# Rotating batch 0 at once, spreading the first weight conversion, and 512-token expert passes after attention

## The chip, the core and the metric

The kernel runs on one core of a Trainium2 chip. The metric is the device time of one execution in microseconds.

## The reference

Attention with rotary embedding, then two feed-forward layers ("expert layers") over the same 2304 tokens. All inputs are float32 but the four weight matrices, which arrive as 64-bit floats.

```
q, k, v: (4 batches, 8 heads, 576 positions, 64)
rotate(x) = concat(x1*cos - x2*sin, x1*sin + x2*cos)
attn = softmax(rotate(q) @ rotate(k).T / 8); o = attn @ v
x  = o.transpose(0, 2, 1, 3).reshape(2304, 512)
h  = x @ w_in1;  x2 = (s * relu(h)**2 + b) @ w_out1      # w_in1 (512, 2048), w_out1 (2048, 512)
h2 = x2 @ w_in2; out = (h2 * sigmoid(1.702 * h2)) @ w_out2
```

## The kernel before

Precision is kept by splitting: each weight, each activation tile x and each hidden tile g is held as a high part and a low part, and each product is made of three matmuls (high by high, high by low, low by high). A weight matrix pair is cut into 16 pieces f of 128 hidden columns; a piece has two halves, m = 0 of `w_in` and m = 1 of `w_out`, 512 KB of 64-bit floats each. `make_half` loads a half into a staging tile and converts it: one ScalarE scaling (L400), three VectorE integer instructions (L401, L402, L405) that put a float32 together out of the two words, a ScalarE cast that gives the high part (L408) and a GpSimd subtraction that gives the low part (L409). Layer 0 keeps 11 converted pieces in SBUF (`HELD`, tags `w0` to `w10`); the other five (`STREAMED`: 2, 5, 8, 11, 14) are converted into one shared buffer (`ws0`, `ws1`), spilled to DRAM and fetched again in every pass. Layer 1 keeps all 16: five in room that is free after attention, the others in the tiles of layer 0's pieces as these are let go.

Work is put into slots. A slot is one score tile of attention; there are 144, 36 for each batch, and some slots below 0 for the preparation. `at(slot, fn)` files a task; a loop at the end goes through the slots, sets a priority of 1000 for each slot, and calls the tasks. The order in which each engine's queue then holds the instructions is laid out by a planner when the kernel is built, by these priorities and a model of when inputs are ready; TensorE's order alone is that of the program (`pin`).

Batch 0 is prepared below slot 0. For each of four head pairs p, and for k and q, `rope_load` fetches a tile `nat` (two buffers shared by all), `rope_cross`, `rope_mul` and `rope_add` rotate it, on GpSimd for k and for most q, on VectorE for q with p < `RV`; `rope_turn` transposes it on TensorE in two groups, splits it into `z` and spills it to DRAM, from where `fetch_pair` brings it back in the layout of the scores. `plan_rope` files pair p's load at slot -16 + 4p and its turns from four slots on. `plan_scales` loads v (`vm`) and makes its scales. The conversion of layer 0's piece f is filed at slot `CONV[0] + CONV[1] * f` = -12 + f.

In a slot, four matmuls make the scores, VectorE copies them out with their minimum (L301), ScalarE takes the exponential, GpSimd normalizes (L321), TensorE transposes, ScalarE and VectorE make the two parts (below slot 20 TensorE and ScalarE, `rest_tile`), and after each four or five slots `weighted` multiplies by v and stores to DRAM (`xT`).

The expert layers run as a generator, `experts`, over passes of 256 tokens: nine for layer 0, nine for layer 1. A step is `first_layer` (FL: 12 matmuls, four chunks by three products, then ScalarE and VectorE make g) or `second_layer` (SL: for layer 0, 12 matmuls of 256 columns; for layer 1, 6 of 512), SL two steps of f behind FL (`SKEW`). From slot 22 on, when the tokens of the first pass are there (`avail`), `target` says how many steps are to be taken in each slot, so that layer 0's passes 0 to 6 lie among attention's slots; the last 512 tokens need the end of attention. Then `widen` gives attention's SBUF and PSUM to the experts, the rest of layer 0 runs, and `refill` converts layer 1's pieces, one for each step, in order of f: the first `EARLY` ones at once, each other one when SL of layer 0's last pass has let a held piece go. `prepare` loads a pass's x and splits it, `finish` copies a pass's sums out and stores them.

## Time and profile before

| | us |
|---|---|
| median of 3 runs (1332.11 to 1335.58) | 1332.78 |
| the profiled execution | 1331.08 |
| its span | 1329.2 |
| TensorE busy | 1133.8 (85%) |
| VectorE busy | 757.0 (57%) |
| ScalarE busy | 684.1 (51%) |
| GpSimd busy | 353.0 (27%) |

The profile is of one execution; times in it count from the start of its span. Busy times are of instructions at work; a matmul's end is modelled, and matmuls are pipelined, so that the distance from one group of matmuls to the next tells more than a matmul's own length. PE is TensorE, PEld its weight load, DVE VectorE, ACT ScalarE, POOL GpSimd, SP the engine whose queue issues the DMAs; L12 is line 12 of the kernel.

### The profile page before, as it was taken

The page shows a single profiled execution, that of the slowest core. Times are in us where ns is not written, and L with a number is a line of the kernel's source. Part 1 is how long each engine was busy: PE and PEld are TensorE (multiplying, and loading weights), DVE is VectorE, ACT ScalarE, POOL GpSimd, SP SyncE. Part 2 cuts the span into 40 slices and gives each one's busy share as a digit, 9 for nine tenths or more (in the row PEclk, how much of TensorE's full clock was granted, in tenths as well). Part 3 has the DMA queues.
Part 4 walks back from the last instruction along what each step waited for, and adds up shares of the span by engine and source line. Part 5 has one row for each costly group of instructions (what it writes and reads, how often), then busy time and mean ns, then how long its engine had stood idle before and what let it go on. Part 6 is the DMA issues. An engine that isn't in the chain of part 4 may idle for free.

```text
span 1329.2 us, 23590 instructions
## 1 busy us (share of the span) xinstructions
PE 1133.8 (85%) x8584; PEld 1046.5 (79%) x8584; DVE 757.0 (57%) x1652; ACT 684.1 (51%) x1483; POOL 353.0 (27%) x350
## 2 busy tenths in 40 slices
PE   0126568998999999899999968987999999999998
PEld 0124448887889889898899968987899999999997
DVE  7888736766566676576665649389333333333322
ACT  2348555666566666566666647566333323332332
POOL 5675644432424343244111113044000000000000
PEclk9998689999989999999999989999999999999999
DMA  7987746657755677475665357566011101100000
GB/s 243 302 278 248 245 137 177 198 169 241 220 166 180 192 247 226 151 210 173 195 212 161 112 168 248 165 223 190 16 33 32 31 2 33 32 17 17 17 17 17
DMA packets 133204, 197.42 MB, mean 149 GB/s; under 512 B 32352, under 2 KB 99424, under 8 KB 133088
## 3 DMA queue, kind: packets, MB, share of 16 engines
q1 hardware_dynamic: 133088, 195.91, 47.8%
q8 instruction: 68, 1.11, 0.4%
q14 instruction: 48, 0.39, 0.1%
HBM read 152.34 MB, written 43.52 MB: 147 GB/s over the span
## 4 chain that ended last, share of the span: by engine, by line
PE 55%; DMA 12%; issue 11%; DVE 10%; ACT 5%; POOL 4%; SPq 2%; DVEq 0%; POOLq 0%; ACTq 0%
PE acc L90 21%; PE l L90 14%; PE l1b L90 7%; PE t L90 4%; PE av L90 4%; PE s L90 4%; DVE P L301 2%; POOL w L409 2%; DMA xT<-pt 2%; DMA vm<-in_v_dram 2%; DMA stage<-in_moe_w_out_dram 2%; DMA xl0b<-xT 1%; DVE pt L344 1%; DMA qb<-qsp 1%; ACT P L310 1%
## 5 line engine op out<-in xcount | busy, mean ns | idle before, releaser
L321 POOL TENSOR_SCALAR P<-P,st 128x576 f32<-128x576 f32 x144 | 113.9, 792 | 344.4 <-DVE st L320 244.7
L90 PE MATMUL acc<-w,gh1b 128*128 128x512 f32 x576 | 202.4, 392 | 0.0
L310 ACT ACTIVATE P<-P,st 128x576 f32<-128x576 f32 x144 | 111.8, 776 | 103.8 <-DVE P L301 103.8
L90 PE MATMUL acc<-gh0b,w 128*128 128x256 f32 x792 | 164.8, 290 | 0.1
L90 PE MATMUL l<-xh0b,w 128*128 128x256 f32 x704 | 145.6, 289 | 14.0 <-ACT r0b L505 8.7
L90 PE MATMUL t<-ident,P 128*128 128x128 f32 x720 | 109.1, 285 | 45.4 <-ACT pt L359 24.8
L301 DVE TENSOR_SCALAR_CACHE_REDUCE P<-s 128x576 f32<-128x576 f32 x144 | 108.5, 753 | 63.5 <-PE s L90 62.2
L90 PEld LDWEIGHTS acc<-gh0b,w 128*128 128x128 f32 x792 | 131.4, 193 | 1.1 <-issue 0.7
L409 POOL TENSOR_TENSOR w<-stage,w 128x512 fp32r<-128x512 f32 x64 | 92.6, 1450 | 145.4 <-ACT w L408 139.6
L90 PEld LDWEIGHTS l<-xh0b,w 128*128 128x128 f32 x704 | 117.9, 195 | 16.0 <-ACT r0b L505 10.4
L90 PEld LDWEIGHTS t<-ident,P 128*128 128x128 f32 x720 | 84.2, 145 | 58.4 <-issue 23.0
L90 PE MATMUL s<-k,qb 128*128 128x288 f32 x640 | 121.3, 317 | 3.9 <-DVE P L301 3.9
L90 PEld LDWEIGHTS acc<-w,gh1b 128*128 128x128 f32 x576 | 108.8, 189 | 19.3
L90 PE MATMUL l<-xh1b,w 128*128 128x256 f32 x576 | 115.1, 283 | 4.4 <-DVE r1b L510 4.4
L90 PE MATMUL l1b<-xh1b,w 128*128 128x256 f32 x576 | 115.1, 283 | 3.7 <-DVE r1b L510 3.7
L344 DVE TENSOR_TENSOR pt<-t,pt 128x640 f16<-128x640 f32 x124 | 101.9, 822 | 28.4 <-ACT pt L342 28.0
L90 PE MATMUL acc<-gl0b,w 128*128 128x256 f32 x396 | 113.1, 286 | 2.9 <-DVE gl0b L514 2.9
L90 PE MATMUL acc<-w,gl1b 128*128 128x512 f32 x288 | 113.8, 395 | 0.0
L342 ACT CAST pt<-t 128x640 f16<-128x640 f32 x144 | 99.0, 688 | 18.6 <-PE t L90 17.4
L90 PEld LDWEIGHTS s<-k,qb 128*128 128x128 f32 x640 | 95.5, 198 | 12.5 <-issue 6.7
L507 ACT ACTIVATE r0b<-r0b,sb 128x256 f32<-128x256 f32 x144 | 86.8, 603 | 33.0 <-DVE r0b L506 32.6
L90 PE MATMUL l<-xl0b,w 128*128 128x256 f32 x352 | 101.5, 288 | 1.4 <-DVE xl0b L479 0.7
(97 smaller groups left out, 2564.5 us busy)
## 6 DMA issues: line engine op xcount, KB each, us to landing
ws<-wd SPq DMA_DIRECT2D x90, 512.0 KB, 4.5
k<-ksp SPq DMA_DIRECT2D x32, 576.0 KB, 5.8
stage<-in_moe_w_in_dram SPq DMA_DIRECT2D x32, 512.0 KB, 4.7
stage<-in_moe_w_out_dram SPq DMA_DIRECT2D x32, 512.0 KB, 4.4
ksp<-z SPq DMA_DIRECT2D x32, 160.0 KB, 4.6
qsp<-z SPq DMA_DIRECT2D x32, 160.0 KB, 4.4
wd<-w SPq DMA_DIRECT2D x10, 512.0 KB, 5.4
vsp<-vz SPq DMA_DIRECT2D x16, 320.0 KB, 4.6
```

The costliest lines, as they stand in the source:

```text
L90: pin(nc.tensor.matmul(*args, **kw))
L301: nc.vector.tensor_scalar(pr.rearrange("p (n s) -> p n s", n=2), ps[:, :, :HS], -Q_SCALE, None, op0=ALU.mult, op1=ALU.min, accum_out=st[:, ...
L310: nc.scalar.activation(pr, pr, AF.Exp, bias=st[:, 0:1], scale=-1.0, accum_out=st[:, 1:2])
L321: nc.gpsimd.tensor_scalar(pr, pr, st[:, 2:3], 1.0, op0=ALU.mult, op1=ALU.mult)
L342: nc.scalar.copy(hi, pc)
L344: nc.vector.tensor_tensor(lo, pc, hi, op=ALU.subtract)
L409: nc.gpsimd.tensor_tensor(lo, f32(low), f32(hi), op=ALU.subtract)
L507: nc.scalar.activation(r, r, AF.Identity, bias=sb[:, 1:2], scale=sb[:, 0:1])
```

## The change

Two things are changed together.

At the start: all tiles of batch 0's rotation are loaded one after the other (pair p at slot -16 + p) and each pair has a tile of its own, `boot`, that holds natural q and k and k's cross products; it lies in the room of weight pieces that are converted later. The turns of pair p are filed at slots 4p - 8 to 4p - 6. `RV` is 3. The conversion of piece f is filed at slot -4 + 2f, its cast and its subtraction one slot later (`WLAG`); the staging tiles of the pieces below 13 lie in the room of the last two held pieces.

After attention: layer 0's last two passes become one of 512 tokens, layer 1 has four passes of 512 and a last one of 256. FL and layer 0's SL then have 512 columns in a matmul. Layer 1 streams pieces 11 and 14 and holds 14, of which three go ahead; a streamed piece is fetched two steps of f ahead (`EARLIER`), and its conversion waits until the shared buffer is let go (`freed[1]`). PSUM has five accumulator banks in a ring and three FL banks (before: six and two).

```diff
-    STREAMED = ((2, 5, 8, 11, 14), ())
+    STREAMED = ((2, 5, 8, 11, 14), (11, 14))
-    EARLY = NF - len(HELD[0])
+    EARLY = len(HELD[1]) - len(HELD[0])
...
+    boot = {}
+    BOOT = (5, 6, 7, 8)
...
+    def boot_part(p, i):
+        return boot[p][:, i * S : (i + 1) * S].rearrange("p (t e i) -> p t e i", t=RT, e=2)
     def rope_load(b, p, which, st):
-        nat = att.tile([128, RT, 2, HD], F32, tag="nat", name=f"nat{b}{p}{which}")
+        if b == 0:
+            if p not in boot:
+                boot[p] = wpool.tile([128, 2048], F32, tag=f"w{BOOT[p]}", name=f"boot{p}")
+            nat = boot_part(p, which)
+        else:
+            nat = att.tile([128, RT, 2, HD], F32, tag="nat", name=f"nat{b}{p}{which}")
...
     def make_half(t, w_in, w_out, f, m, nm):
+        elif f < HELD[0][-2]:
+            if m == 0:
+                stages[0] = wpool.tile(
+                    [128, 2, 512], U64, tag=f"w{len(HELD[0]) - 1 - f % 2}", name=f"stage{nm}"
+                )
+            raw = stages[0][:, m]
...
-        nc.scalar.copy(hi, f32(low))
-        nc.gpsimd.tensor_tensor(lo, f32(low), f32(hi), op=ALU.subtract)
+        def split():
+            nc.scalar.copy(hi, f32(low))
+            nc.gpsimd.tensor_tensor(lo, f32(low), f32(hi), op=ALU.subtract)
+        return split
...
-        make_half(t, *W[layer], f, m, f"{layer}_{f}")
+        split = make_half(t, *W[layer], f, m, f"{layer}_{f}")
+        if layer == 0:
+            at(int(CONV[0] + CONV[1] * f) + WLAG, split)
+        else:
+            split()
...
+        pool = late["acc"] if ring[0] % 5 in (1, 2, 3) else ps_acc
...
+    PASSES = [(0, t, TB) for t in range(0, NT - 2 * TB, TB)] + [(0, NT - 2 * TB, 2 * TB)]
+    PASSES += [(1, t, 2 * TB) for t in range(0, NT - TB, 2 * TB)] + [(1, NT - TB, TB)]
+    LAST0 = [n for n, x in enumerate(PASSES) if x[0] == 0][-1]
...
     def experts():
...
-            while late and len(kept[1]) < NF:
-                f = len(kept[1])
+            while late and turned[0] < NF:
+                f = turned[0]
                 if f in HELD[1]:
                     if HELD[1].index(f) >= freed[0]:
                         break
...
                     if not freed[1]:
                         break
                     freed[1] = 0
-                for m in range(2):
-                    weight(1, f, m)
-                fresh[f] = kept[1][f]
+                fresh[f] = [weight(1, f, m) for m in range(2)]
+                turned[0] += 1
                 return
...
-            if (layer, blk) == (0, NB - 1) and f in HELD[0]:
+            if n == LAST0 and f in HELD[0]:
                 freed[0] += 1
-            if (layer, blk, f) in [(0, NB - 1, NF - 1)] + [(1, 0, x) for x in STREAMED[1]]:
+            if (n, f) in [(LAST0, NF - 1)] + [(LAST0 + 1, x) for x in STREAMED[1]]:
                 freed[1] = 1
...
+                z = f + EARLIER
+                if late and z in STREAMED[layer] and z not in fresh and n != LAST0 + 1:
+                    fetched[z] = fetch_weight(layer, z, f"{n}_")
...
-        gap = 2 if b else 1
         for g in range(2):
-            at(s + 4 + gap * g, rope_turn, b, p, which, g, st)
+            at(s + 4 + 2 * g if b else 4 * p + RT0 - which + g, rope_turn, b, p, which, g, st)
...
-    CONV = (-12, 1.0)
+    CONV = (-4, 2)
+    RT0 = -7
+    WLAG = 1
...
-    RV = 2
+    RV = 3
...
-                r = bounds[b - 1] + RS + 9 * p if b else -RL + 4 * p
+                r = bounds[b - 1] + RS + 9 * p if b else -RL + p
...
-        late["acc"] = ctx.enter_context(tc.tile_pool(name="ps_acc2", bufs=4, space=PSUM))
+        late["acc"] = ctx.enter_context(tc.tile_pool(name="ps_acc2", bufs=3, space=PSUM))
```

## Rows read from the trace of the kernel before

**Rows 1.** Windows: stretch, its length, each engine's busy us (instructions), granted clock, DMA share, GB/s.
```profile
0.00:70.00 70.00, 10.10 (x35) 5.68 (x35) 57.93 (x83) 24.30 (x42) 41.55 (x39) 1.00 0.84 276
70.00:160.00 90.00, 43.27 (x227) 32.12 (x227) 73.90 (x131) 55.13 (x105) 64.60 (x53) 0.83 0.80 257
160.00:192.00 32.00, 18.69 (x153) 14.15 (x151) 11.03 (x40) 18.87 (x36) 14.07 (x16) 0.93 0.64 182
...
217.00:767.00 550.00, 511.71 (x4437) 488.91 (x4436) 355.26 (x885) 346.37 (x764) 180.33 (x204) 0.98 0.63 190
...
794.00:905.00 111.00, 102.41 (x814) 99.87 (x815) 81.15 (x134) 72.27 (x148) 31.53 (x23) 0.98 0.64 211
905.00:936.00 31.00, 22.73 (x154) 20.01 (x153) 28.80 (x44) 18.41 (x38) 11.68 (x10) 1.00 0.58 181
936.00:1324.00 388.00, 387.98 (x2469) 351.90 (x2468) 123.95 (x281) 122.77 (x298) 1.30 (x1) 1.00 0.08 20
```

**Rows 2.** Groups by line, VectorE, 0 to 192 us.
```profile
L402 DVE SCALAR_TENSOR_TENSOR stage<-stage 128x512 uint32<-128x512 uint32 x32 | 34.4, 1075 | 5.7 <-ACT stage L400 4.7
L405 DVE SCALAR_TENSOR_TENSOR stage<-stage 128x512 uint32<-128x512 uint32 x32 | 34.1, 1064 | 0.5
L401 DVE TENSOR_SCALAR stage<-stage 128x512 uint32<-128x512 uint32 x32 | 26.1, 816 | 0.0
```

**Rows 3.** Windows of line L405 alone: VectorE busy us (instructions).
```profile
0.00:70.00 70.00, 15.96 (x14) 1.00 0.84 276
70.00:160.00 90.00, 18.09 (x18) 0.83 0.80 257
```

**Rows 4.** Timeline of TensorE: start, length, what, count, idle time before it.
```profile
56.21 1.11 PE L93 MATMUL r<-ident,nat 128*128 128x128 f32 x4 [9.97 <-POOL nat L205]
...
69.93 1.30 PE L90 MATMUL s<-k,qb 128*128 128x288 f32 x4
...
160.26 1.31 PE L90 MATMUL s<-k,qb 128*128 128x288 f32 x4
...
185.53 0.80 PE L90 MATMUL s<-k,qb 128*128 128x288 f32 x4
191.70 0.58 PE L90 MATMUL l<-xh0b,w 128*128 128x256 f32 x1 [5.37 <-ACT xh0b L478]
```

**Rows 5.** Timeline of GpSimd, the first rotation.
```profile
7.89 1.81 POOL L197 TENSOR_TENSOR rot<-nat,tab 128x288 f32<-128x288 f32 x2 [6.59 <-DMA nat<-in_k_dram]
...
11.36 1.79 POOL L205 TENSOR_TENSOR nat<-nat,rot 128x576 f32<-128x576 f32 x1
```

**Rows 6.** DMA issues, 0 to 192 us: count, KB each, median us to landing.
```profile
stage<-in_moe_w_in_dram SPq DMA_DIRECT2D x16, 512.0 KB, 4.9
...
wd<-w SPq DMA_DIRECT2D x10, 512.0 KB, 5.4
```

**Rows 7.** Timeline of VectorE, the first conversions.
```profile
11.82 1.62 DVE L401 TENSOR_SCALAR stage<-stage 128x512 uint32<-128x512 uint32 x1
...
14.03 0.68 DVE L402 SCALAR_TENSOR_TENSOR stage<-stage 128x512 uint32<-128x512 uint32 x1
14.63 0.41 DVE L401 TENSOR_SCALAR stage<-stage 128x512 uint32<-128x512 uint32 x1
14.97 0.68 DVE L405 SCALAR_TENSOR_TENSOR stage<-stage 128x512 uint32<-128x512 uint32 x1
```

**Rows 8.** Chain that ended last, in layer 1: start, length, what.
```profile
1301.52 1.43 PE l L90 x12
1302.95 1.39 PE acc L90 x6
```

**Rows 9.** Timeline of GpSimd after attention.
```profile
826.86 1.31 POOL L409 TENSOR_TENSOR w<-stage,w 128x512 fp32r<-128x512 f32 x1 [1.67 <-ACT w L408]
863.29 4.24 POOL L409 TENSOR_TENSOR w<-stage,w 128x512 fp32r<-128x512 f32 x3 [35.12 <-ACT w L408]
```

**Rows 10.** Timeline of TensorE, after attention's last matmuls.
```profile
794.26 0.55 PE L90 MATMUL l1b<-xh0b,ws 128*128 128x256 f32 x1 [10.62 <-DMA ws<-wd]
```

More of the change, by code (lines that the diff above doesn't have):

```diff
@@ L400, in make_half @@
         nc.scalar.activation(f32(high), f32(high), AF.Copy, scale=2.0**-112)
-        nc.vector.tensor_scalar(low, low, 29, None, op0=ALU.logical_shift_right)
+        if m in ACT_SHIFT and not late:
+            nc.scalar.activation(low, low, AF.Copy, scale=2.0**-29, bias=-0.5)
+        else:
+            nc.vector.tensor_scalar(low, low, 29, None, op0=ALU.logical_shift_right)
         nc.vector.scalar_tensor_tensor(
@@ L482, with x_tile, acc_tile @@
-    l1_banks = [ps_l1.tile([128, 2, TB], F32, tag="l1", name="l1")]
+    stages = {}
+    def x_tile(nm, z=0):
+        if late and z == 0:
+            return late["m2"].tile([128, 4 * TB], F32R, tag="xc", name=nm, bufs=6)
+        return moe.tile([128, 4 * TB], F32R, tag="xs", name=nm, bufs=4)
+    ring = [0]
+    def acc_tile(nm):
+        if late:
+            ring[0] += 1
+        pool = late["acc"] if ring[0] % 5 in (1, 2, 3) else ps_acc
+        return pool.tile([128, 512], F32, tag="acc", name=nm)
@@ new lines, with prepare @@
+    PASSES = [(0, t, TB) for t in range(0, NT - 2 * TB, TB)] + [(0, NT - 2 * TB, 2 * TB)]
+    PASSES += [(1, t, 2 * TB) for t in range(0, NT - TB, 2 * TB)] + [(1, NT - TB, TB)]
+    LAST0 = [n for n, x in enumerate(PASSES) if x[0] == 0][-1]
+    ready = [0, 0]
+    def prepare(n):
+        layer, t0, T = PASSES[n]
+        assert t0 + T <= ready[layer]
+        src = (xT, x2)[layer][:, t0 : t0 + T].rearrange("(c p) t -> p c t", p=128)
+        per = 4 * TB // T
+        hs, ls = [], []
+        for i in range(NCC // per):
+            cs = slice(i * per, (i + 1) * per)
+            xl = x_tile(f"xl{n}_{i}", n > LAST0 and (n - LAST0) % 2)
+            xh = x_tile(f"xh{n}_{i}", n > LAST0 and (n - LAST0) % 2)
+            xl3, xh3 = (z.rearrange("p (c t) -> p c t", t=T) for z in (xl, xh))
+            nc.sync.dma_start(f32(xl3), src[:, cs])
+            nc.scalar.copy(xh, f32(xl))
+            nc.vector.tensor_tensor(xl, f32(xl), f32(xh), op=ALU.subtract)
+            hs += [xh3[:, c] for c in range(per)]
+            ls += [xl3[:, c] for c in range(per)]
+        return hs, ls
@@ L483, with l1_part @@
+    l1_banks = [ps_l1.tile([128, 512], F32, tag="l1", name="l1")]
     l1_turn = [0]
-    def l1_half():
+    def l1_part(T):
+        if T == 512:
+            l1_turn[0] += 2 - l1_turn[0] % 2
         n = l1_turn[0]
-        l1_turn[0] += 1
-        halves = 2 * len(l1_banks)
-        return l1_banks[n % halves // 2][:, n % 2]
-    def first_layer(layer, blk, f, w, xh, xl):
-        nm = f"{layer}b{blk}{f}"
-        ps = l1_half()
+        l1_turn[0] += T // 256
+        bank = l1_banks[n // 2 % len(l1_banks)]
+        return bank[:, n % 2 * 256 : n % 2 * 256 + T]
@@ L494, in first_layer @@
+    def first_layer(n, f, w, xh, xl):
+        layer, t0, T = PASSES[n]
+        nm = f"{n}_{f}"
+        ps = l1_part(T)
         prods = []
@@ new lines, in first_layer @@
+        for i in range(T // TB):
+            cols = slice(i * TB, (i + 1) * TB)
+            r = moe.tile([128, TB], F32, tag="r", name=f"r{nm}{i}")
+            if layer == 0:
+                nc.scalar.activation(r, ps[:, cols], AF.Relu)
+                nc.vector.tensor_tensor(r, r, r, op=ALU.mult)
+                nc.scalar.activation(r, r, AF.Identity, bias=sb[:, 1:2], scale=sb[:, 0:1])
+            else:
+                nc.scalar.activation(r, ps[:, cols], AF.Tanh, scale=0.851)
+                nc.vector.scalar_tensor_tensor(
+                    r, r, 1.0, ps[:, cols], op0=ALU.add, op1=ALU.mult
+                )
+            nc.scalar.copy(gh[:, cols], r)
+            nc.vector.tensor_tensor(gl[:, cols], r, f32(gh[:, cols]), op=ALU.subtract)
@@ L519, in second_layer @@
+        return gh, gl
+    def second_layer(n, f, w, gh, gl, banks):
+        layer, t0, T = PASSES[n]
+        if layer == 0:
+            per = 512 // T
             for c in range(NCC):
@@ L527, in second_layer @@
         else:
-            for c in range(TB // 128):
+            for c in range(T // 128):
                 cs = slice(c * 128, c * 128 + 128)
@@ L608, in experts @@
                 refill()
-                if nxt in ready and nxt not in ahead and f >= NF - 3:
-                    ahead[nxt] = prepare(*nxt)
+                if n + 1 < len(PASSES) and n + 1 not in ahead and f >= NF - 3:
+                    nl, nt, nT = PASSES[n + 1]
+                    if nt + nT <= ready[nl] and (n + 1 < LAST0 or late):
+                        ahead[n + 1] = prepare(n + 1)
         while hist:
@@ L760 @@
     widen()
-    ready.update((0, x) for x in range(NB))
+    ready[0] = NT
     for _ in steps:
```

154 lines of the change are left out of this document (70 added, 84 removed).

## The prediction

> **What bounds the kernel now.** I first cut the span into stretches by busy time [rows 1]. In the last one, 936 to 1324 us, TensorE is busy 388.0 of 388 us at the full granted clock: only fewer or cheaper matmuls help there. In 217 to 767 it is busy 511.7 of 550 us, with VectorE at 355.3 of 550 (65%) beside it. The room is at both ends. Up to 192 us TensorE is busy 10.1 + 43.3 + 18.7 = 72.1 us, so 120 us are lost, while VectorE works 57.9 of the first 70 us and 73.9 of the next 90, and the DMA engines are at 0.84 and 0.80 of their time. From 794 to 936 us TensorE idles 8.6 + 8.3 = 16.9 us.
>
> Then I asked what VectorE does up to 192 us: the conversion of the first layer's weights, L401, L402 and L405 32 times each, costs 26.1 + 34.4 + 34.1 = 94.6 us, or 2.96 us for a half (one of the 32 weight pieces) [rows 2]; 14 halves are done by 70 us and 18 more by 160 us [rows 3]. TensorE's order of work shows what that delays [rows 4]: the third pair's turn waits 9.97 us until 56.2 for GpSimd's rotation, and the first score comes at 69.9. Score 15 stands at 160.3, so the first slots cost 90.3/15 = 6.0 us; scores 15 to 23 take 25.3 us, 3.2 us a slot, with no conversion left beside them [rows 3, 4]. The experts start at 191.7 us. That start, not the first score, is the one that moves the rest, since what follows is near TensorE's own work.
>
> **The start.** All eight rotations of batch 0 now run in the first slots, from tiles of their own (boot); only two pairs instead of three are turned ahead of slot 0; and the conversion of f stands at slot 2f - 4 instead of f - 12. None of it is removed. What counts is how much still has to be done before slot 22, where the experts start.
>
> VectorE: 142.9 us of work stand before 192 us [rows 1]. Weights 13, 14 and 15 now come at slots 22, 24 and 26: 6 halves x 2.96 = 17.7 us leave. RV = 3 moves one rotation from GpSimd to VectorE: it costs GpSimd 5.3 us (7.89 to 13.15) [rows 5]; on VectorE I take 3 us, between nothing and that. 142.9 - 17.7 + 3 = 128.2 us. At the share of the first 160 us, 131.8/160 = 0.82, that is done at 156 us.
>
> DMA: 276 GB/s over 70 us, 257 over 90 and 182 over 32 make 48.3 MB [rows 1]. Six halves of 0.52 MB and the two of the ten spills that belong to f = 14 [rows 6] leave: 44.1 MB, at the first stretch's 276 GB/s 160 us, at the mean of both 166.
>
> The two agree. I take 160 us, 32 earlier. Checked by slots: the second pair's turns were over 9.97 us before 56.2, at 46 [rows 4]; with less conversion ahead of them in VectorE's queue an estimate for the first score is 40 us; 22 slots at 5.2 us, nearer to 6.0 than to 3.2 because a half still falls on each, and 6 us for the first tokens' way through DRAM make 160. Bounds: with VectorE and DMA at full share (44.1 MB at 276/0.84) 128 to 134 us, never approached here, so I go half way, 147 us, a gain of 45; at the other end the first slots keep all their cost and nothing is gained.
>
> What is late next: the 17.7 us of conversion now fall into slots 22 to 27, where VectorE has a third of its time free. Its cover is TensorE's own work; without it they cost all 17.7 us, with it nothing; I charge 5. The one shared buffer of the streamed weights is late too: weight 14's conversion, spill and the fetch of 5 must pass through it between the experts' steps 2 and 5. A spill lands in 5.4 us [rows 6]; three such moves are about 15 us against three steps of about 6, so I price it at nothing, at most 5. SP's queue carries all of these loads: the eight rotation loads now stand ahead of the loads of v. They are 8 x 128 x 576 x 4 B = 2.4 MB, 9 us at 276 GB/s; v's scales are not needed before slot -4, and the wait falls on weight loads that no one needs yet. Start: 32 - 5 = 27 us gained.
>
> The conversion's price rests on a neighbour. L401 took 0.41 us at 14.63, when GpSimd was idle, and 1.62 us at 11.82, while GpSimd's addition ran from 11.36 to 13.15 [rows 5, 7]; a half with no such neighbour is about 0.41 + 0.68 + 0.68 = 1.8 us, a mean one 2.96. The Trainium skill (SBUF — State Buffer, Who interferes with whom) says that VectorE instructions which take the port pair shared with GpSimd contend with it under an exclusive lock: whichever starts first holds it for the whole instruction and the other blocks. The trace agrees: 0.41 against 1.62 us. The rule speaks against the change, since conversions move among the slots' GpSimd normalizations; what it would do is in the third rival.
>
> **After attention.** Twelve 256-column matmuls take 1.43 us, six 512-column ones 1.39 [rows 8]. In four 512-token passes of the second layer, 16 f each, 24 narrow ones (2.86) become 12 wide (2.78): 64 x 0.08 = 5.1 us. In the first layer's last pass 48 narrow ones (5.72) become 24 wide (5.56): 16 x 0.16 = 2.6. Together 7.7 us; this needs no waiting to go away.
>
> The 16.9 us of gaps: GpSimd ends the tenth half at 828.2 and starts the next three at 863.3 [rows 9]. Five weights have room of their own, the sixth must wait until the last block of the first layer lets go of its weights, and then 22 halves are pressed into the stretch in which VectorE is at 28.8 of 31 us [rows 1]. In the new kernel the last pass covers 512 tokens, so the weights fall free one by one over about 16 x 5.56 = 89 us instead of 46, and three instead of five go ahead. VectorE has time for them there, and each step gives twice the time for the chain from a first product to the second. I take 12 of the 16.9 us back; ends 0 and 16.9. Not taken back: the 10.62 us at 794.26 [rows 10], the way out of attention, which stands in both; the first tokens there are now two loads of 512 KB instead of one, charged 2 us. The streamed weights 11 and 14 of the second layer are 2 MB a pass in 89 us against 0.08 DMA share [rows 1], fetched two steps ahead: hidden; without that cover 4.9 us for each [rows 6]. Five accumulator banks for passes that need four: a bank's copy has one 2.8 us step to be done; nothing, or 2 us a pass. After attention: 7.7 + 12 - 2 = 17.7, say 18.
>
> **Sum.** 27 + 18 = 45. The profiled execution took 1331.08 us (span 1329.2 and 1.9 around it), 1.7 under the median of 1332.78: 1331.1 - 45 = 1286 us.
>
> **Rivals.** *The start gains nothing much.* The conversion is shifted, not removed, and VectorE and DMA are as full as they were; the experts start at 185. For it: 0.82 and 0.8 shares; against it: 192 minus 160 us in which both fall off. 1331 - 7 + 5 - 18 = 1311 us. Chance 0.17.
>
> *The late gaps stay.* Weight 14 of the second layer can be converted only when the first pass has retired 11, immediately ahead of its use: load 4.9, conversion 3, casts and subtraction some 3, so 11 us for a single time, and the gaps' 12 us stay as waits for banks or VectorE. For it: conversion in order, one weight at a time; against it: in the trace three halves were prepared ahead and ran back to back at 863.3 [rows 9], so the load and VectorE's part don't wait. 1331 - 27 - 8 + 11 = 1307 us. Chance 0.12.
>
> *Slower: conversion among the slots costs more than ahead of them.* One mechanism, at VectorE's queue in slots 0 to 22: scores, norms and casts queue behind halves that GpSimd's work lengthens, and the first score stays at 70. At 6.0 us a slot the experts start at 70 + 132 + 6 = 208: 1331 + 16 + 5 - 18 = 1334; at 7 us, 1356. It decides from 6.1 us a slot; for it: 6.0 was seen with 18 halves in 15 slots [rows 3, 4]; against it: the new plan has one a slot, and a first score at 40 needs 7.4 us. Chance 0.09. [...]
>
> *No effect:* the planner fills idle queues with whatever is ready, and so may order the start as before, and the late gaps cancel the 7.7 us. Chance 0.03.
>
> **Numbers.** The forecast has 0.59, its own range 1265 to 1300. Best ends: 45 at the start, 7.7 + 16.9 late, 1331 - 70 = 1261, so the low end is 1260. The high end takes in the first two rivals with a little more, 1320. Faster than by 0.3% (about what a measurement of this kernel tells from no change): 0.88 less a little of the first rivals' tails, 0.87; same 0.04; slower 0.09.
>
> **What would show it.** Right: first score at about 40 us, experts at about 160, conversions still running beside them; no weight piece after 790 waiting for room as long as 35 us, TensorE idle under 7 us in the 140 us after 794; the last stretch's pairs at 2.78 us. Wrong: a first score near 70, slots of 6 us or more, or new idle time of TensorE beside f = 11 and 14 of the second layer or at the turn of passes. What would break it most is the planner's order, which no row of before can show.

## The result and the profile after

The changed kernel took 1317.8 us (median of 4 runs, 1313.0 to 1321.3) beside 1332.4 for the kernel before (4 runs): a ratio of 0.990, interval 0.986 to 0.9935. It is faster by about 14 us, where 45 were forecast. The profiled execution took 1318.1 us (span 1316.3), 13.0 less than the one of before.

Windows of the changed kernel, columns as in [rows 1]:

```profile
0.00:70.00 70.00, 14.15 (x52) 9.71 (x52) 49.87 (x67) 13.79 (x26) 44.74 (x43) 0.97 0.53 165
70.00:160.00 90.00, 52.91 (x286) 39.35 (x285) 56.38 (x128) 59.87 (x114) 34.92 (x33) 0.65 0.82 261
160.00:192.00 32.00, 13.48 (x75) 9.31 (x75) 26.66 (x48) 17.82 (x32) 21.41 (x21) 0.68 0.82 258
...
217.00:767.00 550.00, 508.89 (x4412) 486.00 (x4412) 361.94 (x892) 349.45 (x770) 188.04 (x209) 0.98 0.64 197
785.00:927.00 142.00, 121.81 (x579) 99.94 (x578) 99.87 (x171) 86.44 (x183) 39.92 (x28) 0.92 0.56 186
927.00:1311.00 384.00, 384.00 (x1780) 321.34 (x1779) 128.54 (x297) 123.99 (x313) 6.21 (x5) 1.00 0.16 48
```

Up to 70 us VectorE works 49.9 us and the DMA engines 0.53 of their time; before it was 57.9 us and 0.84 [rows 1]. From 70 to 160 VectorE falls from 73.9 to 56.4 us. The timeline of TensorE:

```profile
21.09 1.11 PE L91 MATMUL r<-ident,boot 128*128 128x128 f32 x4 [21.09 <-POOL boot L216]
...
51.18 1.09 PE L91 MATMUL r<-ident,boot 128*128 128x128 f32 x4 [8.80 <-POOL nat L213]
...
58.56 1.31 PE L88 MATMUL s<-k,qb 128*128 128x288 f32 x4
...
191.66 0.58 PE L88 MATMUL l<-xh,w 128*128 128x256 f32 x1 [6.38 <-ACT xh L522]
...
789.07 2.23 PE L88 MATMUL av<-pt,vf 128*64 128x320 f16 x30
...
803.37 0.55 PE L88 MATMUL l<-xh,ws 128*128 128x256 f32 x1 [10.44 <-DMA ws<-wd]
...
881.15 4.82 PE L88 MATMUL acc<-g,w 128*128 128x512 f32 x12 [2.52 <-ACT g L566]
...
921.78 1.32 PE L88 MATMUL acc<-w,g 128*128 128x512 f32 x3 [1.88 <-ACT y L599]
925.67 2.93 PE L88 MATMUL acc<-w,g 128*128 128x512 f32 x6 [2.57 <-ACT y L599]
```

The first score comes at 58.6 us instead of 69.9 [rows 4], but the experts start at 191.66, as before (191.70). From there to attention's last product it takes 597.4 us (789.07 - 191.66), before 588.1: the start has won nothing, and the stretch behind it has become 9.3 us longer. From the first product after attention (803.37) TensorE needs 507.9 us to its end at 1311.3; before, from 794.26 [rows 10] to its end at 1324.0, 529.7. So 21.8 us are gained after attention, 9.1 lost by its end: 12.7, and the profiles differ by 13.0.

Windows of the 50 us that follow the experts' start, first before, then after, show where the 9.3 us go:

```profile
191.70:241.70 50.00, 43.83 (x363) 40.71 (x364) 29.85 (x75) 28.85 (x64) 16.77 (x18) 0.95 0.50 147
191.66:241.66 50.00, 38.13 (x277) 34.22 (x277) 35.81 (x69) 27.00 (x56) 21.68 (x20) 0.83 0.64 211
```

TensorE does 277 matmuls there instead of 363. In 217 to 767 the two kernels go at the same pace (511.7 us busy before [rows 1], 508.9 after).

VectorE's line L425 (L405 before [rows 3]) shows the conversion's pace, a count for each half:

```profile
0.00:70.00 70.00, 4.07 (x4) 0.97 0.53 165
70.00:160.00 90.00, 13.80 (x16) 0.65 0.82 261
160.00:192.00 32.00, 4.92 (x6) 0.68 0.82 258
```

Four halves are done by 70 us, not 14. What happened instead stands in the timelines of SP's queue, of GpSimd and of VectorE, shown in this order:

```profile
11.39 0.38 SPq L408 DMA_DIRECT2D stage<-in_moe_w_in_dram  x1
12.14 0.62 SPq L196 DMA_DIRECT2D nat<-in_k_dram  x1
12.88 0.36 SPq L196 DMA_DIRECT2D nat<-in_q_dram  x1
...
24.33 7.18 SPq L237 DMA_DIRECT2D ksp<-z  x2
...
42.70 8.96 SPq L236 DMA_DIRECT2D qsp<-z  x2
...
65.45 0.51 SPq L413 DMA_DIRECT2D stage<-in_moe_w_out_dram  x1
```
```profile
42.29 1.28 POOL L431 TENSOR_TENSOR w<-stage,w 128x512 fp32r<-128x512 f32 x1
43.54 1.39 POOL L216 TENSOR_TENSOR boot<-boot,rot 128x576 f32<-128x576 f32 x1
44.89 1.39 POOL L213 TENSOR_TENSOR nat<-nat,tab 128x576 f32<-128x576 f32 x1
46.25 1.52 POOL L208 TENSOR_TENSOR rot<-nat,tab 128x288 f32<-128x288 f32 x2
47.74 1.39 POOL L216 TENSOR_TENSOR nat<-nat,rot 128x576 f32<-128x576 f32 x1
49.09 1.39 POOL L213 TENSOR_TENSOR nat<-nat,tab 128x576 f32<-128x576 f32 x1
```
```profile
9.21 3.94 DVE L208 TENSOR_TENSOR rot<-boot,tab 128x288 f32<-128x288 f32 x4 [5.31 <-DMA boot<-in_q_dram]
13.08 3.21 DVE L213 TENSOR_TENSOR boot<-boot,tab 128x576 f32<-128x576 f32 x2
...
41.93 8.57 DVE L159 TENSOR_SCALAR vrow<-vrow 1x8 f32<-1x8 f32 x1
...
50.85 0.23 DVE L230 TENSOR_TENSOR z<-r,z 64x128 fp32r<-64x128 f32 x1
```

Three things are to be seen. Batch 0 no longer uses the two shared `nat` tiles, so batch 1's first pair is loaded into them at 12 us and rotated on GpSimd among batch 0's rotations; five of the seven instructions in the rows of GpSimd belong to that pair (those that read or write `nat`). GpSimd works without a pause from 30.2 to 50.5 us; a VectorE instruction on 1x8 numbers, started in the midst of that at 41.93, took 8.57 us and ended as the run ended; TensorE's wait of 8.80 us at 51.2 stands behind it, for the split of a turn (L230) comes soon after it in VectorE's queue and ends at 51.1. (The profile books that wait on GpSimd's L213, which ended at 50.5.) And SP stands 7.2 and 9.0 us at spills of z that wait for VectorE's part of the turns, with no weight load issued between 11.4 and 65.5 us.

### The profile page after: what moved, and what is told of

Read it like the earlier page. It is cut to its first block, busy times and chain, and to the rows that moved or that the text cites. A ratio compares the mean times of both kernels' runs of the same rounds, so it can differ in the third digit from the quotient of the medians.

```text
span 1316.3 us, 21001 instructions
## 1 busy us (share of the span) xinstructions
PE 1130.4 (86%) x7432; PEld 997.1 (76%) x7432; DVE 750.2 (57%) x1656; ACT 675.6 (51%) x1483; POOL 343.9 (26%) x346
## 3 DMA queue, kind: packets, MB, share of 16 engines
q1 hardware_dynamic: 131456, 201.15, 48.8%
## 4 chain that ended last, share of the span: by engine, by line
PE 54%; DMA 16%; DVE 12%; issue 6%; ACT 5%; SPq 4%; POOL 3%; DVEq 0%; POOLq 0%; ACTq 0%
PE l L88 21%; PE acc L88 21%; DMA stage<-in_moe_w_in_dram 5%; PE av L88 4%; PE s L88 3%; PE t L88 3%; DMA xT<-pt 2%; DVE P L312 2%; SPq L271 2%; DMA xl<-xT 2%; DVE stage L421 2%; ACT P L321 1%; DVE stage L422 1%; DVE pt L355 1%; DMA stage<-in_moe_w_out_dram 1%
## 5 line engine op out<-in xcount | busy, mean ns | idle before, releaser
L88 PE MATMUL l<-xh,w 128*128 128x256 f32 (+1 forms) x1280 | 330.8, 331 | 15.3 <-ACT r L558 7.6
L88 PEld LDWEIGHTS l<-xh,w 128*128 128x128 f32 x1280 | 225.2, 191 | 39.3 <-ACT r L558 10.4
L88 PE MATMUL l<-xl,w 128*128 128x256 f32 (+1 forms) x640 | 212.1, 331 | 2.2 <-DVE xl L523 2.2
L88 PE MATMUL acc<-w,g 128*128 128x512 f32 x696 | 169.4, 392 | 4.5 <-ACT y L599 4.5
L88 PEld LDWEIGHTS acc<-w,g 128*128 128x128 f32 x696 | 131.2, 189 | 32.8 <-ACT y L599 5.6
L88 PE MATMUL t<-ident,P 128*128 128x128 f32 x720 | 111.5, 289 | 50.9 <-ACT pt L370 28.4
L88 PEld LDWEIGHTS l<-xl,w 128*128 128x128 f32 x640 | 122.3, 191 | 14.2 <-DVE xl L523 2.7
L88 PE MATMUL acc<-gh,w 128*128 128x256 f32 x616 | 130.0, 294 | 0.0
L560 ACT ACTIVATE r<-r,sb 128x256 f32<-128x256 f32 x144 | 86.1, 605 | 42.5 <-DVE r L559 42.1
L567 DVE TENSOR_TENSOR g<-r,g 128x256 fp32r<-128x256 f32 x160 | 71.0, 448 | 64.7 <-ACT g L566 64.7
L88 PEld LDWEIGHTS acc<-gh,w 128*128 128x128 f32 x616 | 103.2, 195 | 0.7 <-issue 0.7
```

The lines of the kernel that those rows point to most:

```text
L88: pin(nc.tensor.matmul(*args, **kw))
L560: nc.scalar.activation(r, r, AF.Identity, bias=sb[:, 1:2], scale=sb[:, 0:1])
L567: nc.vector.tensor_tensor(gl[:, cols], r, f32(gh[:, cols]), op=ALU.subtract)
```

## The experiments

"After" is the changed kernel. Each was timed beside the kernel before on its own chip, so the ratio to it counts; times of the three events are from its profile. `start_noconv` and `late_noconv` leave out a part of the work.

| run | median us | ratio to before, interval | first score | experts | last product of attention |
|---|---|---|---|---|---|
| after | 1317.8 | 0.990, 0.986 to 0.9935 | 58.6 | 191.7 | 789.1 |
| start_only | 1339.4 | 1.007, 1.003 to 1.010 | 58.4 | 189.6 | 790.5 |
| late_only | 1305.8 | 0.981, 0.977 to 0.985 | 69.6 | 192.2 | 780.1 |
| stagger | 1304.8 | 0.978, 0.974 to 0.983 | 50.8 | 183.2 | 774.8 |
| no_spread | 1312.8 | 0.986, 0.981 to 0.990 | 69.1 | 197.3 | 784.3 |
| hold_b1 | 1307.9 | 0.985, 0.982 to 0.988 | 50.9 | 189.0 | 778.4 |
| spill_act | 1313.6 | 0.989, 0.983 to 0.995 | 58.2 | 189.3 | 791.8 |
| all_dve | 1301.2 | 0.981, 0.976 to 0.985 | 50.4 | 173.4 | 768.0 |
| loads_at_once | 1316.2 | 0.991, 0.988 to 0.994 | 61.8 | 194.9 | 785.6 |
| hold_dve | 1304.2 | 0.983, 0.981 to 0.985 | 48.6 | 183.1 | 774.0 |
| stagger_dve | 1300.9 | 0.979, 0.976 to 0.981 | 48.8 | 178.7 | 769.2 |
| stagger_vpool | 1324.5 | 0.995, 0.993 to 0.997 | 82.6 | 205.9 | 800.9 |
| start_noconv | 1303.3 | 0.983, 0.980 to 0.987 | 40.6 | 180.4 | 768.7 |
| start_twice | 1330.5 | 1.003, 1.001 to 1.005 | 48.5 | 191.5 | 804.6 |
| act_free | 1316.1 | 0.987, 0.983 to 0.991 | 49.6 | 183.6 | 782.1 |
| split256 | 1317.3 | 0.991, 0.989 to 0.994 | 69.9 | 189.8 | 778.0 |
| late_noconv | 1293.8 | 0.974, 0.971 to 0.977 | 69.5 | 191.3 | 779.0 |
| stage4 | 1296.9 | 0.978, 0.976 to 0.980 | 48.5 | 177.6 | 764.6 |
| late_shift | 1299.0 | 0.974, 0.970 to 0.978 | 49.4 | 179.3 | 768.3 |

**The two parts, and the start's two.** `late_only` has the new expert layers with the start of before; `start_only` the other way round; `stagger` is after with batch 0's loads, tiles, rotations and turns put back; `no_spread` is after with the conversion's old slots.

```diff
 # late_only: after, start of before; start_only: before, start of after.
 # The lines of the start as start_only changes them; late_only changes them back:
-    CONV = (-12, 1.0)
+    CONV = (-4, 2)
-        nat = att.tile([128, RT, 2, HD], F32, tag="nat", ...)
+        if b == 0: ... nat = boot_part(p, which)
+        elif f < HELD[0][-2]: ... raw = stages[0][:, m]
+            at(int(CONV[0] + CONV[1] * f) + WLAG, split)
 ...
 # stagger: after, with the rotation of before
-        if b == 0: ... nat = boot_part(p, which)
+        nat = att.tile([128, RT, 2, HD], F32, tag="nat", ...)
-                r = ... else -RL + p
+                r = ... else -RL + 4 * p
-    RV = 3
+    RV = 2
 ...
 # no_spread: after
-    CONV = (-4, 2)
+    CONV = (-12, 1.0)
```

> The new kernel with the start of the old one (rotation staggered from shared tiles, conversion at f - 12, RV = 2); 512-token passes kept. The two traces put the first expert matmul at 191.70 us before and 191.66 after, attention's last product at 779.78 and 789.07, and the stretch from the streamed piece's matmul (794.26, 803.37) to the end of TensorE's work at 529.7 and about 507.6 us. Theory: the parts add, the start lost 9 us and the late part won 22: 1332.4 - 22 = 1310 us. Rival, the forecast's: the start won, the late part won 18 and something between them was lost: then this kernel stands at 1314 or above.

> The old kernel with the start of the new one alone; 256-token passes as before. Theory (parts add, the start loses): 1332.4 + 9 = 1341 us, first score at 58, experts at 192. Rival, the forecast's: the start wins 27 us when nothing late stands beside it: 1305. Third: no effect of the start at all, 1332.

> The new kernel with only the rotation put back (shared tiles, pair p at slot -16 + 4p, turns four slots on, RV = 2); conversion spread over two slots a piece as in the change. If the rotation at once is what costs at the start (VectorE and GpSimd both at it, first turn at 21.1 instead of 13.2 us, an 8.6 us VectorE instruction at 41.9), it comes back to 1310 us. If the spread conversion costs (weight loads and conversions in the slots, SP's queue full from 60 to 135 us), it stays at 1318.

> The new kernel with only the conversion's slots put back (piece f at slot f - 12); rotation at once kept. If the spread is what costs, 1310 us; if the rotation at once costs, 1318. If both cost, this and the kernel with the rotation put back lie between the two.

The new expert layers alone win 25 us, the new start alone loses 9; together that is 16, and 14 to 15 were measured. With the rotation put back and the conversion spread, the ratio goes from 0.990 to 0.978 (intervals apart), some 15 us. With the conversion's old slots and the rotation at once it is 0.986, which the intervals do not tell from `late_only` (0.981) nor from after. So rotating at once is what costs, shown beside the spread conversion; spreading the conversion costs nothing by itself (0.978 against 0.981).

**What rotating at once costs.** Four changes to after, one each.

```diff
 # hold_b1: batch 1's first load ordered behind batch 0's value loads
+        if b == 1 and p == 0:
+            pin(ins, "V")
 # spill_act: batch 0's z spilled from ScalarE's queue
-                nc.sync.dma_start(rows[:, :, 0:320], zz[0:64])
+                (nc.sync if b else nc.scalar).dma_start(rows[:, :, 0:320], zz[0:64])
 # all_dve
-  eng = nc.vector if b == 0 and (p < RV and which == 0) else nc.gpsimd
+  eng = nc.vector if b == 0 else nc.gpsimd
 # loads_at_once: tiles of their own and early loads stay, rotations and turns as before
-        at(s, rope_load, b, p, which, st)
+        at(s if b else s - 3 * p, rope_load, b, p, which, st)
-                r = ... else -RL + p
+                r = ... else -RL + 4 * p
 ...
```

> The changed kernel with one thing more: the load of batch 1's first pair is held, in SP's order, behind the last value load of batch 0, so that its rotation on GpSimd (9.3 us, 33.3 to 50.5 us in the changed kernel) leaves the start. Theory A (batch 1's first rotation slipped into the start, because batch 0 no longer uses the two shared tiles): batch 0's last turns come 8 us earlier, the first score at about 51 instead of 58.6, and most of the 13 us that the rotation at once costs come back, about 1307 us. Theory B (the spills of z at the head of SP's queue hold the weight loads): the spills wait a little less, 1312 to 1316. Theory C (GpSimd and VectorE hold each other up while both rotate): little changes, 1314 to 1318, since batch 0's own eight rotations still run side by side.

> The changed kernel, but batch 0's z is spilled to DRAM from ScalarE's queue instead of SP's. In the changed kernel SP stood 19.9 us at three of these spills before 52 us (7.2 + 3.8 + 9.0), and no weight load was issued between 11.4 and 65.5 us. Theory B (SP's queue holds the weight loads): weight loads run on between 20 and 50 us, the DMA share there rises from 0.30 to 0.6 or more, the experts start at 180 or earlier, and about 10 us come back, 1308. Theory A and theory C: the weight loads were waiting for their staging tiles, which GpSimd lets go late, so nothing moves by more than 3 us, 1315 to 1320.

> The changed kernel, but all eight rotations of batch 0 are on VectorE and none on GpSimd. Theory C (side by side each is slowed by the other): a rotation that has VectorE for itself costs less than the 3.4 us that each took side by side (10.5 us for three), some 2.5 us by the fastest rows, eight of them 20 us, so that all are done by 35 us instead of 45; the first score at about 45, total about 1305. Theory A: batch 1's first rotation still runs on GpSimd, but no longer in the way of batch 0's, so it too expects most of it back, 1307. Theory B: spills wait less, since z comes earlier, 1308 to 1312. Against all three: VectorE, which the conversion needs, gets 13 us more work, and the total stays at 1318 or goes above.

> The changed kernel with tiles of its own for each pair and with the loads at once, but the rotations themselves and the turns filed four slots apart for each pair, as before, and two instead of three rotations on VectorE. Theory D (the eight loads ahead of v's and the weights' cost the time): stays at 1317. Theory C (the rotating at once costs): back to the 1305 of the kernel with the rotation put back. Theory A (batch 1's first pair finds the shared tiles free and is rotated early): that pair still slips in, so 1312 to 1317, with a first score no earlier than 56.

Theory A holds for what it names. With batch 1's first pair held back, the 1x8 instruction took 0.79 us, SP's spill at 42.9 us 1.26 instead of 8.96, and the turn that had waited 8.80 us started at 43.5 instead of 51.2, by the timeline of TensorE in `hold_b1`:

```profile
43.53 1.09 PE L91 MATMUL r<-ident,boot 128*128 128x128 f32 x4 [1.02 <-POOL w L433]
```

The first score came at 50.9, the 51 expected. The ratio went from 0.990 to 0.985 (the intervals just overlap), somewhat under half of what rotating at once costs. Of the 7.7 us won at the first score only 2.6 arrived at the experts' start; how the rest of the gain came about is not shown. Theory C holds as far as the price of a rotation goes: with all eight rotations on VectorE they cost less each, by the timeline of `all_dve`:

```profile
7.41 1.56 DVE L208 TENSOR_TENSOR boot<-boot,tab 128x288 f32<-128x288 f32 x4 [3.54 <-DMA boot<-in_k_dram]
8.89 0.75 DVE L213 TENSOR_TENSOR boot<-boot,tab 128x576 f32<-128x576 f32 x1
...
10.96 0.75 DVE L216 TENSOR_TENSOR boot<-boot 128x576 f32<-128x576 f32 x1
```

A rotation with GpSimd idle is 2 x 0.39 + 0.75 + 0.75 = 2.3 us; in after, beside GpSimd's own, L208 took 0.98 and L213 1.6 us. The Trainium skill (SBUF — State Buffer, Who interferes with whom) has VectorE instructions with two SBUF inputs contend with GpSimd's reads, and the one that comes second block; the traces agree in that the instruction takes longer beside GpSimd: 0.39 against 0.98 us. To within the intervals all of the loss came back (0.981 against the 0.978 of `stagger`), though the first score came at 50.4 and not at the 45 expected. By the time alone theory A would do as well, since it too expected most of the loss back: with GpSimd free of batch 0's rotations the 1x8 instruction took 0.26 us.

Theory B fell: with the spills on ScalarE's queue the wait moved with them, and the time stayed. Nor were weights loaded earlier: no weight load was issued between 11.1 and 60.4 us, and the DMA share of 20 to 50 us is 0.30, as in after. ScalarE in `spill_act`:

```profile
42.41 8.93 ACTq L237 DMA_DIRECT2D qsp<-z  x2
52.01 0.59 ACT L229 CAST z<-r 128x512 fp32r<-128x512 f32 x1 [9.63 <-PE r L91]
```

`loads_at_once` stays at after's time with rotations filed four slots apart. That is what theory D expected and what theory A allows; the number does not tell them apart. Its trace speaks for A: GpSimd's order is again line by line over all pairs (first turn at 20.5 us, as in after), batch 1's pair is again among them, and the 1x8 instruction again takes 7.00 us. Tiles of their own with their data there are enough for the order to be laid out so; the slots in which rotations are filed don't hold it.

```diff
 # hold_dve: after + hold_b1 + all_dve        # stagger_dve: stagger + all_dve
 # stagger_vpool: stagger, batch 0's value loads from GpSimd's queue
-                ins = nc.sync.dma_start(
+                ins = (nc.sync if b else nc.gpsimd).dma_start(
```

> The changed kernel with both repairs: all eight rotations of batch 0 on VectorE, and the load of batch 1's first pair held behind batch 0's value loads. If the two repair the same loss (GpSimd and VectorE side by side in the first 50 us), they don't add: 1300 to 1304, as with VectorE's rotations alone. If batch 1's early rotation costs by itself even where batch 0 is not on GpSimd (it stands before the subtractions of the first weights there, 31.9 to 49.6 us), another 5 us go: 1296.

> The kernel with the rotation put back, but all eight rotations of batch 0 are on VectorE, 2.3 us each by the rows of the kernel that had them all there at once. Theory C (GpSimd's rotation and VectorE's conversion hold each other up): VectorE gets six rotations or 14 us more, and saves more than that in conversions at 1.8 instead of 2.6 us, so the first score comes at about 42 instead of 50.8 and the total is 1297 to 1300. Rival, theory F (the slots set the pace): the start of the experts moves by less than 4 us, 1302 to 1308. Against both: VectorE's queue is the bound and the total goes to 1310.

> The kernel with the rotation put back (spread conversion, new expert layers), and batch 0's value loads, ten small DMAs for each pair, issued from GpSimd's queue instead of SP's. Theory E (in the first slots SP's queue sets the pace: SP is busy 24 to 25 of each 30 us from 30 to 90 us, some 0.6 us for each issue, and a pair brings some 40 issues): ten of 40 leave, 6 us for each of three pairs, so the experts start 15 to 18 us earlier, 165 to 168 instead of 183, and the total falls to about 1292. Rival, theory F (the conversion's slots, two for each piece, and the chain load, conversion, subtraction set the pace): the experts start within 4 us of 183 and the total stays at 1302 to 1308. A third: GpSimd's issues cost more than SP's and stand in front of the rotations and the norms: later than 183, 1310 or more.

The two repairs are the same loss: both at once give 0.983, not told from 0.981 and 0.985. `stagger_dve` is 0.979, as `stagger`: the first score came 2.0 us earlier (42 was expected, 48.8 measured), and 4.5 us won at the experts' start are too few to be told here. `stagger_vpool` took the third way: GpSimd issues 20 value loads in 11.6 us up to 37.1 us, the second pair's rotation stands among and behind them, its turn starts on TensorE at 49.1 instead of 28.6 us, and the first score comes at 82.6. It says nothing on SP's queue as the pace.

**What sets the 133 us from the first score to the experts.** Two changes to after, one to `stage4` (below).

```diff
 # start_noconv: L421, L422, L425 left out for layer 0 (cast and subtraction read the scaled word)
 # start_twice: each load of a first-layer half issued twice
+        for _ in range(1 if late else 2):
 # act_free: stage4, layer 0's scaling on VectorE, its cast on GpSimd (layer 1's stay)
-        nc.scalar.activation(f32(high), f32(high), AF.Copy, scale=2.0**-112)
+        nc.vector.tensor_scalar(f32(high), f32(high), 2.0**-112, None, op0=ALU.mult)
-            nc.scalar.copy(hi, f32(low))
+            nc.gpsimd.tensor_copy(hi, f32(low))
```

> The changed kernel, but the first layer's weights are not put together: VectorE's three instructions for each half are left out (and the scaling has another factor), so these weights are other numbers; loads, casts, subtractions, spills and their slots stay. Some 70 us of VectorE leave the stretch up to the experts. Theory H (VectorE's conversion sets the pace of the first slots, as the prediction's sum of VectorE's work has it): the 133 us from the first score to the experts shrink by 20 us or more, total 1295 or less. Rival, theory I (DMA: loads, spills and fetches, at 0.8 of the DMA engines' time, set it): they shrink by less than 8 us, 1308 to 1316.

> The changed kernel, but each load of the first layer's weights is issued twice into the same tile: 26 halves before the experts, 13.6 MB more, at the 250 GB/s of the first slots 54 us of DMA. Theory I (DMA sets the pace): the experts start 30 to 54 us later and the total is 1345 to 1370. Theory H (VectorE's conversion): less than 15 us later, 1318 to 1333; the second load of a half adds its 5 us to the way of each piece, which has two slots or 10 us.

> The kernel with staggered rotation on VectorE and four staging tiles (1296.9, ratio 0.978, experts at 177.6), with the first layer's conversion taken off ScalarE: the scaling is on VectorE, the cast on GpSimd. From 45 to 190 us ScalarE stood there 29.7 us at its head of queue for conversions (19.6 for VectorE's part, 10.1 for loads), and TensorE 37.2 us for ScalarE's copies of the transposed scores. Theory K (these waits in ScalarE's queue set the pace of the first slots): the 129 us from the first score to the experts shrink to 100 to 115, the total falls by 8 to 15, 1282 to 1290. Rival, theory L (the pace is that of the way of each pair through DRAM and SP's queue, some 40 issues of 0.6 us for a pair): they stay at 122 to 132, and the total at 1292 to 1300. Against both: the cast and the subtraction on GpSimd and the scaling on VectorE hold each other up, the total rises above 1300.

Without VectorE's conversion the stretch became 139.8 us long, with doubled loads 143.0, with ScalarE freed of the conversion 134.0. Windows of `start_noconv` show VectorE nearly idle while the slots go no faster:

```profile
75.00:100.00 25.00, 13.48 (x70) 9.89 (x70) 5.37 (x18) 13.39 (x27) 7.42 (x8) 0.57 0.76 229
100.00:150.00 50.00, 30.99 (x178) 24.20 (x177) 15.34 (x47) 33.26 (x64) 23.36 (x25) 0.67 0.89 291
```

Theories H and K are refuted; in `act_free` the third outcome came, a total above 1300. Theory I fits only in part: the doubled loads moved the experts' start by nothing, since the first score came 10 us earlier and the stretch became 10 us longer, where 30 to 54 were expected. Their windows show 0.93 of DMA time from 100 to 150 us, and attention ended 15.5 us later than in after. `start_noconv` won 18 us at the first score (40.6) and 11 at the experts.

The pace of these slots stays open. Not tried is a shorter way of each pair through DRAM (spill, fetch, value loads: some 40 issues of about 0.6 us on SP's queue). The clock is a rival that no run separates: over 70 to 160 us the granted clock is 0.65 in after and 0.83 before [rows 1]. But the first three slots of the kernel before took 9.4 us each, from 69.9 to 98.1 us, at a granted clock of 1.00, so a low clock alone does not make slots slow.

**After attention.** Two changes to `late_only`, then `stage4` and `late_shift`.

```diff
 # split256: each 512-column matmul of a 512-token pass as two of 256
+            for z in range(2):
+                mm(o[:, half], a, bb[:, half], ...)
 # late_noconv: VectorE's three instructions left out for layer 1
 # stage4: stagger_dve
-            raw = late["m2"].tile(..., bufs=3)
+            raw = late["m2"].tile(..., bufs=4)
 # late_shift: stage4
-        if m in ACT_SHIFT and not late:
+        if late and m == 0:
```

> The kernel with the new expert layers alone, but each 512-column matmul of the 512-token passes is issued as two of 256 columns. The second layer's other matmuls, wide already before, and all tiles, passes and orders stay. By the prediction's sum this gives back the whole gain of width: 7.7 us of 25, so 1313. If instead the gain lies mostly in having half as many groups (each hand-over from one group of matmuls to the next costs some 0.06 us: 12 of 256 columns 1.43 us, 6 of 512 1.39, 12 of 512 2.72, so 0.114 and 0.222 for a matmul), 24 in a group take 2.80 instead of 2.72 us and 96 such groups give back the same 7.7 us, and the hand-overs' part, another 9 us, stays gained. If all of the 17 us that the passes became shorter is width, it goes to 1323. So 1323 against 1313 tells whether width or hand-overs made the larger part.

> The kernel with the new expert layers alone, but the second layer's weights are not put together: the three VectorE instructions of each half are left out (and the scaling has another factor), so its weights are other numbers; loads, casts, subtractions, spills and all waits for room stay. It shows what VectorE's part of the conversion still costs after attention. Theory G (the 12 us of gaps that the prediction took back are still lost to conversion, as waits of TensorE for casts and sums behind VectorE and ScalarE): the waits at f = 11 to 15 and at the first turn of passes go, 5 to 8 us faster than the kernel with the conversion, 1298 to 1300. Rival: the waits are those of banks and of the way through DRAM and stay: 1304 to 1307.

> The kernel with staggered rotation, all on VectorE, with one thing more: four instead of three staging tiles for the second layer's conversion. Theory J (the conversion after attention goes from load to load: a staging tile is let go, 5 us of load, then scaling, three VectorE instructions, cast and subtraction; the waits of 0.6 to 2.2 us at the later pieces come from it): with a load more in flight the waits shrink and 2 to 5 us are gained, 1296 to 1299. Rival (VectorE's own work is what is short in those stretches): nothing, 1299 to 1303.

> The kernel with staggered rotation on VectorE and four staging tiles, but in the second layer the shift of each first half (one of VectorE's three instructions, some 0.7 us) is on ScalarE. Theory M (VectorE's own work is what the conversion after attention still lacks; leaving its three instructions out gained 10.6 us): 14 to 16 of 90 instructions leave VectorE, 1 to 3 us gained, 1294 to 1296. Rival (ScalarE, on which TensorE's waits of 0.6 to 2.2 us are booked, has no room either): nothing or up to 4 us slower, 1296 to 1301.

The chains that ended last, of after and of `split256`:

```profile
939.77 2.72 PE l L88 x12
942.49 2.72 PE acc L88 x12
```
```profile
916.99 2.87 PE l L88 x24
919.86 2.75 PE acc L88 x12
```

24 narrow matmuls in one group take 2.87 us, twice the 1.43 of two groups of 12 [rows 8], so hand-overs between groups cost nothing and the second explanation in the expectation falls. Twelve wide ones take 2.72. From its first product after attention `split256` needs 517.4 us and `late_only` 509.0, with idle time of 6.1 and 11.1 us in 795 to 930: 8.4 us in time, and 13.4 us of width if the 5.0 us by which the waits differ are added back. The 96 groups of the prediction's sum at 2.87 less 2.72 us make 14.4. The windows of `late_only` and of `late_noconv` over that stretch:

```profile
795.00:930.00 135.00, 123.92 (x542) 101.13 (x543) 102.63 (x176) 86.57 (x186) 40.98 (x28) 0.94 0.57 186
```
```profile
795.00:930.00 135.00, 131.81 (x597) 109.89 (x596) 52.05 (x100) 90.48 (x198) 37.05 (x28) 0.97 0.57 187
```

With VectorE's part left out the idle time falls from 11.1 to 3.2 us and the ratio from 0.981 to 0.974, some 10 us: theory G, by more than it expected. Of the 11.1 us, 6.2 are waits for g (ScalarE's cast and VectorE's subtraction); they are gone, so they were VectorE's conversion. Another 4.7 us are waits for ScalarE's copies of layer 0's sums out of the accumulator banks; 3.2 of these stay, so the rival is right for the banks at the turn to layer 1. One more staging tile (`stage4`, 0.978 against 0.979) and a moved shift (`late_shift`, 0.974) change nothing that the intervals can tell. These two are the fastest that leave no work out: by their ratios 16 to 21 us under after.

## Why the prediction was wrong

*The start, +27 forecast, -9 measured.* The step that failed is "at the share of the first 160 us, 0.82, that is done at 156 us". The work was sized well: VectorE did 49.9 + 56.4 + 26.7 = 132.9 us by 192 us (128.2 forecast), with 26 halves and not 32. But its share was 132.9/192 = 0.69. Work filed later left VectorE and DMA with nothing to do instead of letting what follows move up: in the first 70 us for the waits shown above, later because the stretch from the first score to the experts is 120 to 143 us long in every kernel run here, with VectorE's conversion or without. Taking that out (`start_noconv`) moves the experts by 11 us, through the first score alone; so neither of the two sums that "agreed" at 160 measured what sets that start. They were two sums of busy time on queues that wait for something else.

The check by slots failed where it could be seen: 40 us for the first score, measured 58.6 (18.6 of the 31.7 missed), and 5.2 us a slot, measured (191.7 - 58.6 - 6)/22 = 5.8. For the first score the prediction counted less conversion ahead of the second pair's turns, and not what newly free tiles let in: batch 1's pair. Holding that pair back won 7.7 us of the 18.6, leaving out VectorE's conversion 18.0; the two were not tried together.

The prediction also took the experts' start as "the one that moves the rest". `all_dve` starts the experts 18.8 us before `late_only`, which has the start of before, and ends attention 12.1 us before it, but the ratios are 0.981 both. Of the kernels that leave no work out and spread the conversion or rotate at once, none is faster than `late_only` clear of the intervals, so whether a repaired start is worth anything in total is not shown.

*Late conversion, -5 forecast:* the sign is right for after, 9.3 us, but the price is not that of the conversion alone. From the experts' start to attention's end the kernels with the old conversion slots (before, `late_only`, `no_spread`) take 587 to 588 us and after 597.4. Others that spread it take 587.1 (`stage4`) to 602.5 us (`spill_act`). Without VectorE's conversion (`start_noconv`) it is 588.3, but the experts also start 11 us earlier there. What makes the difference among those that spread it is not shown.

*After attention, +18 forecast, 21.8 measured; both terms were mis-sized.* Width was put at 7.7 us, with 2.78 us for twelve wide matmuls, from a group of six in another product; a wide group took 2.72 and `split256` prices width at 13.4. Of the gaps 12 us were to come back: TensorE's idle time after its first product went from 16.9 [rows 1] to 9.8 us (123.63 - 113.88 in 803.4 to 927), 7 back, and the longest wait left a slower group behind it. The chain named, room and conversion of layer 1's pieces, is right: GpSimd's pause of 35.12 us between two subtractions [rows 9] has become 8.45 at most, and what is left is in the main VectorE's conversion (`late_noconv`). The banks, put at nothing or 2 us a pass, cost 4.5 us once, at the turn to layer 1: the waits of 1.88 and 2.57 us at 921.8 and 925.7 in the timeline above, for ScalarE's copies of the sums (L599). The second x load, 2 us, cost nothing: the way out of attention is 10.44 us, before 10.62.

*The rivals.* "The start gains nothing much" (1311) came nearest: the experts start where they did. But its reason, VectorE and DMA as full as they were, is not what happened: both were emptier, VectorE at 0.69 of its time up to 192 us and the DMA engines at 0.53 of theirs up to 70. That its number is near is in part luck. The slower rival named the right pair of engines, VectorE held up by GpSimd, but not the place: it happened before slot 0, among rotations, and not through the norms in the slots. "The late gaps stay" is half true. Weight 14 of the second layer made no wait of its own.

## What to carry to other kernels

When work is moved out of a stretch, ask of the stretch's end which wait it follows, and test that by leaving the work out: a sum of busy time over a share bounds the end only where the engine is the one that others wait for. When tiles are given to one user, look at who gets the tiles that he leaves, since work of a later stage may come in early and stand in a queue. Price an instruction from rows of its own shape and product.

## What the hardware showed

- A VectorE instruction on 1x8 numbers took 8.57 us (0.15 in the kernel before at the same place, 0.79 in `hold_b1`), while GpSimd worked seven instructions without a pause, from 42.29 to 50.48 us. It happened in after, `start_only` and `spill_act` (8.57 each) and in `loads_at_once` (7.00), each time with batch 1's rotation in GpSimd's run. That rotation does not always bring it: with batch 1's pair rotated early as well, the instruction took 1.50 us in `start_twice` and 1.87 in `no_spread`. Larger VectorE instructions got their turn between two of GpSimd's; why this one did not, no run here shows. The Trainium skill (SBUF — State Buffer, Who interferes with whom) says that of two instructions that contend for the shared ports the one issued first has them for its whole length and the other is blocked. If that is what happened here, the trace goes beyond it: VectorE's instruction lasted through seven of GpSimd's.
- After a wait of 2.52 us, twelve wide matmuls took 4.82 us instead of 2.72 (881.2 us in after). The granted clock over 881.2 to 885.9 us is 0.64, so most of that time at the lower of its two levels (1.2 GHz); over 860 to 878, with TensorE busy 17.7 of 18 us, and over 886 to 890 it is 1.00 (2.4 GHz).
- With the weight loads doubled the first score came earlier, 48.5 instead of 58.6 us, with the queues' instructions laid out in another order; which part of that order did it is not shown.
